# First keys and queries loaded in three pieces of heads, a planner with transfers at 270 GB/s, and inverse sums of two blocks also on ScalarE

## The chip, the cores and the metric

The program runs on one core of a Trainium2 chip. The metric is the time of one execution on the device in microseconds (us). The kernel before took 1215.35 us (median of three runs, 1214.6 to 1215.85). The execution that the profiler recorded took 1215.45 us; the trace of its instructions spans 1213.3 us of them, so 2.15 us lie outside the trace.

## What is computed

Three stages follow one another, each on the output of the stage before:

```python
# 1. attention in chunks: batch 4, heads 8, 768 tokens, head width 64, 8 memory tokens
for c in range(nc):                       # a chunk has 32 queries
    k_full = concat([mem_k, k[l_start:r_end]])      # 16 keys to the left, 8 to the right
    scores = scale * q_c @ k_full.T
    a = exp(scores - max(scores)); a = a / (sum(a) + 1e-9)
    out[c] = a @ v_full
x = out as (3072 tokens, 512)
# 2. first layer:  h = x @ w_in (512 x 2048); g = h * tanh(softplus(h)); x1 = g @ w_out
# 3. second layer: the same shapes, with g = h * sigmoid(1.702 h)
```

The weights come as 64-bit floats and are turned into 32-bit numbers on the chip.

## The kernel before

**Blocks.** Tokens are worked on in blocks of 384. Block `j` has 8 *quads* of attention: a quad is two heads by two groups of 96 queries. For blocks 0 and 1 (`EARLY = 2`) keys and queries are loaded with the tokens in the partitions (`rows_of_heads`, one call for four quads: all 8 heads of two groups of 96 queries) and turned on TensorE (`turned`, L665). Of each quad, in this order: TensorE turns queries and keys (L673) into a bank `h`; ScalarE or VectorE copies the bank to `qT` or `kT` (L680, L681); TensorE forms the scores (L708); VectorE adds the mask and finds the extreme (L721); ScalarE takes the exponential and the sums (L736); VectorE inverts the sums (L754, L758) and multiplies by them (`norm`, L761); TensorE turns the result (L782); it is copied to `aT` (L788, L789); TensorE multiplies by the values `vt` (L799 in block 0, L808 in later blocks); the output is split into a high and a low part, `xh` and `xl` (L834 to L840), the input of the first layer.

**First layer.** `step(j, f)` does one of 16 slices of the inner width: 12 matmuls into a bank `h` (L895, called the *first product* of slice `f` below), the activation on ScalarE (L907), and the products with `w_out` into four banks `o` (L924). Within block 0 the weights are still being converted: of each half of a slice ScalarE or VectorE takes the high word (L343, L346), and VectorE does three more steps (L352, L356, L360) and for `w_in` the split (L379, L384). The turned keys and the first products share two banks `h`. A weight load waits until the conversion six halves earlier has begun (`AHEAD`).

**Second layer.** `step2` does 7 products of 6 matmuls per pair of slices (L1057), with tanh on ScalarE (L1107), one step on VectorE (L1109) and the products of L1084.

**What sets the order.** Nothing is written in the order in which it runs. Every operation is added to a `Plan` with a rank, its reads and writes, and one or more *ways* (an engine, a duration, the function). `Plan.issue` (L139) then plays the program through with these durations: at each moment each free engine takes, of the operations whose inputs are there, the one of lowest rank. ScalarE takes first what needs no other activation table, and an operation that does (`other`) only when nothing else is ready. A transfer ends at `max(bus, end + 0.65) + size`, and its readers may start 0.9 later; `size` comes from `bus()`, 360 GB/s for runs of 512 bytes or more and half of it for shorter ones. The operations are then written out in the order of these planned starts, and on the chip each engine works through its own list strictly in that order, waiting where an input is not there yet. Transfers are issued by SyncE (SP); those of block 0's keys, queries and values may also be issued by GpSimd (POOL). SP's list is worked off in order as well, and a transfer that finds the queue full waits at its head.

Of the kernel before, what the change touches and what calls it, by code (L numbers as in the profile page):

```python
# [12 lines left out]
AF = mybir.ActivationFunctionType  # L13
# [5 lines left out]
EARLY = 2  # L19
# [62 lines left out]
class Plan:  # L82
# [2 lines left out]

    LAG = {"pe": 0.2, "act": 0.16, "dve": 0.13, "pool": 0.2}
    RELOAD = 1.4

    def __init__(self):
        self.ops = []  # L90
# [48 lines left out]
    def issue(self):  # L139
        engines = ("pe", "act", "dve", "pool", "sp")  # L140
        free = dict.fromkeys(engines, 0.0)
        ready = {e: [] for e in engines}
        load = dict.fromkeys(engines, 0.0)
        coming = []
        bus = 0.0
        for op in self.ops:
            if op.need == 0:
                heapq.heappush(coming, (0.0, op.seq, op))
            op.start = None
        left = len(self.ops)  # L150
        now = 0.0
        table = None
        order = []
        while left:
            while coming and coming[0][0] <= now + 1e-9:
                op = heapq.heappop(coming)[2]
                for w, (e, dur, *_) in enumerate(op.ways):
                    heapq.heappush(ready[e], (op.rank, op.seq, w, op))
                load[op.ways[0][0]] += op.ways[0][1]
            for e in engines:  # L160
                if free[e] > now + 1e-9:
                    continue
                kept = []
                pick = other = None
                while ready[e]:
                    item = heapq.heappop(ready[e])
                    op, w = item[3], item[2]
                    if op.start is not None:
                        continue
                    if w:  # L170

                        e0, d0 = op.ways[0][:2]
                        if max(free[e0] - now, 0.0) + load[e0] - d0 < op.ways[w][1] - d0 + 0.3:
                            kept.append(item)
                            continue
                    if e == "act" and op.table not in (None, table):

                        if other is None:
                            other = item
                        else:  # L180
                            kept.append(item)
                        continue
                    pick = item
                    break
                if pick is None:
                    pick = other
                elif other is not None:
                    kept.append(other)
                for item in kept:
                    heapq.heappush(ready[e], item)  # L190
                if pick is None:
                    continue
                op, w = pick[3], pick[2]
                e_, dur, fn, *size = op.ways[w]
                op.start, op.way = now, w
                load[op.ways[0][0]] -= op.ways[0][1]
                order.append(op)
                left -= 1
                end = now + dur
                if e == "act" and op.table not in (None, table):  # L200
                    if table is not None:
                        end += self.RELOAD
                    table = op.table
                free[e] = end
                lag = self.LAG.get(e, 0.0)
                if size:
                    bus = max(bus, end + 0.65) + size[0]
                    end, lag = bus, 0.9
                for o, far in op.after:
                    t = end + lag if far else (now + 0.01 if not size else now + 0.01)  # L210
                    o.at = max(o.at, t)
                    o.need -= 1
                    if o.need == 0:
                        heapq.heappush(coming, (o.at, o.seq, o))
            times = [coming[0][0]] if coming else []
            times += [free[e] for e in engines if free[e] > now + 1e-9]
            if not times:
                assert not left, "operations wait for one another"
                break
            now = min(t for t in times if t > now) if any(t > now for t in times) else now  # L220
        order.sort(key=lambda o: (o.start, o.seq))
        for op in order:
            op.ways[op.way][2]()


def dve(n, fast=False):
    return (170 + (0.53 if fast else 1.04) * n) / 1000


def act(n, psum=False):  # L230
    return ((180 if psum else 220) + 0.86 * n) / 1000


def bus(nbytes, run):
    return nbytes / 360e3 * (1 if run >= 512 else 2)


@with_exitstack
def kernel(
# [13 lines left out]
    nc = tc.nc  # L253
    B, H, S, D = q.shape
    NT, DM = out.shape
    DFF = w1_in.shape[1]
    NM = mem_k.shape[2]
    CHUNK, LEFT, RIGHT = 32, 16, 8
    P = 128
    KD = DM // P  # L260
    NF = DFF // P
    TB = 384
    NB = NT // TB
    GQ = 96
    NG = S // GQ
    GB = TB // GQ
    WIN = P - NM
# [6 lines left out]
    scale = 1.0 / float(D) ** 0.5  # L274
# [6 lines left out]
    add = plan.add  # L281
# [227 lines left out]
    ident = fixed(sb.tile([P, P], F32, name="ident"))  # L509
# [16 lines left out]
    def rows(src, r0, dims, col, width):  # L526

        return bass.AP(
            tensor=src.tensor, offset=src.offset + r0 * D + col, ap=[[st * D, n] for st, n in dims] + [[1, width]]
        )  # L530
# [91 lines left out]
        load(rank, vt, parts, P * GB * HV * D * 4, 256)  # L622
        return vt

    def windows(src, mem, b, t0, h0, nh, tile, i):


        runs = [(0, WIN, t0, 0, nh)]
        if b == 0 and h0 == 0 and t0 < 0:
            runs = [(0, WIN, t0, 1, nh - 1), (-t0, WIN + t0, 0, 0, 1), (0, -t0, 0, 0, 1)]  # L630
        elif b == B - 1 and h0 + nh == H and t0 + WIN > S:
            runs = [
                (0, WIN, t0, 0, nh - 1), (0, S - t0, t0, nh - 1, 1), (S - t0, t0 + WIN - S, t0, nh - 1, 1)
            ]
        parts = [
            lambda row=row, n=n, t=t, h=h, c=c: (
                tile[row:row + n, i, h:h + c],
                rows(src, (b * H + h0 + h) * S + t, [(1, n), (S, c)], 0, D),
            ) for row, n, t, h, c in runs
        ]  # L640
        parts.append(lambda: (tile[WIN:P, i], rows(mem, (b * H + h0) * NM, [(1, NM), (NM, nh)], 0, D)))
        return parts

    def rows_of_heads(j, gp, rank):

        b, s0 = divmod(j * TB, S)
        n = NF - 4 + 2 * j + gp
        qs, ks, vt = (T[nm].new([P, 2, H, D], F32) for nm in (f"wi{n}", f"wo{n}", "vt"))
        kp, vp = [], []
        for i in range(2):  # L650
            t0 = s0 + (2 * gp + i) * GQ - LEFT
            kp += windows(k, mem_k, b, t0, 0, H, ks, i)
            vp += windows(v, mem_v, b, t0, 0, H, vt, i)
        qp = [
            lambda i=i: (
                qs[:GQ, i], rows(q, b * H * S + s0 + (2 * gp + i) * GQ, [(1, GQ), (S, H)], 0, D)
            ) for i in range(2)
        ]
        size = P * 2 * H * D * 4
        load(rank - 4, ks, kp, size, 256, early=j == 0)  # L660
        load(rank - 4, qs, qp, size * GQ // P, 256, early=j == 0)
        load(rank - 2, vt, vp, size, 256, early=j == 0)
        return qs, ks, vt

    def turned(j, hp, st, rank):  # L665
        qs, ks, _ = st
        t = T["h"].new([P, 2 * (GQ + P)], F32)
        qk = T["qT" if hp % 2 else "kT"].new([P, 2 * (GQ + P)], F32)

        def turn():  # L670
            for i in range(2):
                for src, n, c in ((qs, GQ, i * GQ), (ks, P, 2 * GQ + i * P)):
                    nc.tensor.transpose(  # L673
                        t[:, c:c + n], src[:n, i, 2 * hp:2 * hp + 2].rearrange("p h d -> p (h d)"), ident[:n, :n]
                    )

        n = 2 * (GQ + P)
        add(rank, [("pe", 0.4, turn)], reads=[qs, ks, ident], writes=[t])
        add(rank, [
            ("act", act(n, True), lambda: nc.scalar.activation(out=qk[:, :n], in_=t.get(), func=AF.Copy)),  # L680
            ("dve", dve(n), lambda: nc.vector.tensor_copy(out=qk[:, :n], in_=t.get())),  # L681
        ], reads=[t], writes=[qk])
        return (
            lambda d, i: qk[d, i * GQ:(i + 1) * GQ],
            lambda d, i: qk[d, 2 * GQ + i * P:2 * GQ + (i + 1) * P],
            [qk],
        )

    def quad(j, hp, gp, heads, rank):
# [74 lines left out]

        add(rank + 1.4, [("dve", 0.23, plus)], reads=[sm], writes=[r])
        add(rank + 1.4, [("dve", 0.16, inverse)], updates=[r])
        add(rank + 1.4, [("dve", dve(4 * P), norm)], reads=[r, done], updates=[e])

        return after, e

# [484 lines left out]
```

## Time and profile before

| What | Value |
|---|---|
| median of 3 runs | 1215.35 us (1214.6 to 1215.85) |
| profiled execution, its span | 1215.45 us, 1213.3 us |
| TensorE (PE) busy | 1183.9 us, 98%, 6656 matmuls |
| its weight loads (PEld) | 1082.8 us, 89% |
| VectorE (DVE) busy | 822.5 us, 68% |
| ScalarE (ACT) busy | 564.9 us, 47% |
| GpSimd (POOL) busy | 10.1 us, 1% |
| mean granted clock of TensorE | 0.989 of 2.4 GHz |

How to read it: a busy share is an average over the whole span. A row of the windows gives, for a stretch, how long each engine was busy (and with how many instructions), the granted clock of TensorE (1.00 is 2.4 GHz, 0.50 is 1.2 GHz) and what the 16 DMA engines moved. A row of the waits says which engine stood still at which line, until which engine was done with what: total us, times, longest. A row of the timeline gives a start, a duration, and in brackets the idle time before it and what ended it. A bank or tile keeps its name without its number.

### The profile page before, as it was taken

To read this page: it belongs to the slowest core of one execution; us is meant where nothing else is said; L and a number is where in the kernel's file an instruction comes from. 1 tells how busy PE (TensorE), PEld (TensorE's weight loads), DVE (VectorE), ACT (ScalarE), POOL (GpSimd) and SP (SyncE) were. 2 spreads that over 40 slices of the span, in tenths; PEclk is the share of its full clock that TensorE was granted. 3 is DMA by queue.
4 is the path that set the end of the run, shared out by engine and by line. 5 is a ranking of instruction groups with operands and counts; after the bars stand their busy time and mean duration, and the time that the engine had idled before them with its cause. 6 is when DMAs were issued, how large, how long until landed. Compare 5 with 4: busy or idle time off the path is not lost.

```text
span 1213.3 us, 19142 instructions
## 1 busy us (share of the span) xinstructions
PE 1183.9 (98%) x6656; PEld 1082.8 (89%) x6656; DVE 822.5 (68%) x2379; ACT 564.9 (47%) x1303; POOL 10.1 (1%) x27
## 2 busy tenths in 40 slices
PE   7689999999999999999999999999999999999998
PEld 6567789999999999999999998998889888988897
DVE  5798878776866767667665668877655855555554
ACT  4677666655555555655533344445212521232112
POOL 1000000000000000000000000000000000000000
PEclk8799999999999999999999999999999999999999
DMA  9965545533433333334212676699656865566521
GB/s 204 262 216 168 147 124 139 147 94 80 114 88 92 98 91 93 103 81 116 60 49 74 229 257 209 231 356 335 214 186 194 296 226 189 179 224 214 181 106 53
DMA packets 214687, 197.80 MB, mean 163 GB/s; under 512 B 133496, under 2 KB 176519, under 8 KB 214591
## 3 DMA queue, kind: packets, MB, share of 16 engines
q1 hardware_dynamic: 214239, 195.82, 53.0%
q0 software_dynamic: 352, 0.75, 0.4%
q8 instruction: 53, 0.87, 0.3%
q14 instruction: 43, 0.35, 0.1%
HBM read 148.29 MB, written 48.23 MB: 162 GB/s over the span
## 4 chain that ended last, share of the span: by engine, by line
PE 93%; DMA 3%; SPq 2%; DVE 1%; ACT 1%; issue 0%; ACTq 0%
PE h L895 22%; PE o L924 22%; PE h L1057 19%; PE o L1084 15%; PE s L1084 7%; PE s L808 3%; PE s L708 3%; SPq L299 2%; PE s L782 2%; DMA vt<-in_v_dram 1%; DMA wo<-in_moe_w_out_dram 0%; DMA wi<-in_q_dram 0%; DMA x1d<-ev 0%; DMA st<-w1d 0%; DMA w1d<-u 0%
## 5 line engine op out<-in xcount | busy, mean ns | idle before, releaser
L895 PE MATMUL h<-xh,wi 128*128 128x384 f32 x1024 | 269.0, 344 | 5.9 <-ACT qT L680 4.4
L924 PE MATMUL o<-gh,wo 128*128 128x384 f32 x896 | 240.6, 349 | 0.0
L895 PEld LDWEIGHTS h<-xh,wi 128*128 128x128 f32 x1024 | 184.3, 189 | 13.2 <-ACT qT L680 5.2
L895 PE MATMUL h<-xl,wi 128*128 128x384 f32 x512 | 172.9, 338 | 0.0
L924 PEld LDWEIGHTS o<-gh,wo 128*128 128x128 f32 x896 | 158.0, 188 | 2.8
L924 PE MATMUL o<-gl,wo 128*128 128x384 f32 x448 | 150.8, 337 | 0.0
L907 ACT ACTIVATE u<-h 128x384 f32<-128x384 f32 x112 | 55.0, 491 | 132.0 <-PE h L895 125.5
L736 ACT ACTIVATE e<-e,mx 96x128 f32<-96x128 f32 x240 | 94.0, 393 | 23.5 <-DVE mx L721 22.9
L944 DVE TENSOR_TENSOR gl<-u,gh 128x384 fp32r<-128x384 f32 x177 | 96.9, 554 | 11.4 <-ACT gh L939 8.6
L895 PEld LDWEIGHTS h<-xl,wi 128*128 128x128 f32 x512 | 96.7, 189 | 0.0
L1057 PE MATMUL h<-wi,wi 128*128 128x384 f32 x480 | 94.4, 337 | 0.0
L1057 PEld LDWEIGHTS h<-wi,wi 128*128 128x128 f32 x480 | 85.5, 188 | 4.9 <-ACT v L1124 0.2
L924 PEld LDWEIGHTS o<-gl,wo 128*128 128x128 f32 x448 | 84.1, 188 | 0.0
L1124 ACT ACTIVATE v<-h 128x384 f32<-128x384 f32 x61 | 29.9, 490 | 113.2 <-PE h L1057 113.2
L1084 PE MATMUL o<-wo,gh 128*128 128x512 f32 x262 | 82.1, 394 | 0.2 <-ACT ev L951 0.2
L721 DVE CUSTOM_DVE_ANT_0 e<-s,mask 96x128 f32<-96x128 f32 x240 | 55.7, 283 | 37.5 <-PE s L708 36.4
L1057 PE MATMUL h<-wo,wi 128*128 128x384 f32 x384 | 77.2, 336 | 0.0
L907 ACT ACT_TABLE_LOAD x55 | 70.6, 1283 | 10.6 <-PE h L895 9.9
L1107 ACT ACTIVATE u<-e 128x384 f32<-128x384 f32 x64 | 33.5, 524 | 85.2 <-DVE e L1130 85.1
L736 ACT ACT_TABLE_LOAD x54 | 69.3, 1283 | 6.7 <-DVE mx L721 5.8
L1057 PEld LDWEIGHTS h<-wo,wi 128*128 128x128 f32 x384 | 68.2, 188 | 3.0 <-DVE u L1109 0.2
L836 DVE CAST xh<-s 64x192 fp32r<-64x192 f32 x84 | 29.8, 355 | 50.9 <-PE s L808 41.6
(195 smaller groups left out, 2057.8 us busy)
## 6 DMA issues: line engine op xcount, KB each, us to landing
wi<-w2c SPq DMA_DIRECT2D x72, 512.0 KB
wo<-w2o SPq DMA_DIRECT2D x48, 512.0 KB
w2c<-wi SPq DMA_DIRECT2D x24, 512.0 KB
st<-x1d SPq DMA_DIRECT2D x56, 192.0 KB
wi<-in_moe_w_in_dram SPq DMA_DIRECT2D x16, 512.0 KB
wo<-in_moe_w_out_dram SPq DMA_DIRECT2D x16, 512.0 KB
st<-in_moe_w_in_dram SPq DMA_DIRECT2D x16, 512.0 KB
w2d<-v SPq DMA_DIRECT2D x32, 256.0 KB
```

The lines of the kernel that those rows point to most:

```text
L708: nc.tensor.matmul(out=s[hh][:, i, :], lhsT=queries(d, i), rhs=keys(d, i), start=True, stop=True,)
L721: nc.vector.tensor_tensor_reduce(out=e[:, i, hh, :], in0=s[hh][:, i, :], in1=mask[:GQ, mask_of(g0 + i), :], scale=-scale, scalar=-NEG, op0 ...
L736: nc.scalar.activation(out=e[:, i, hh, :], in_=e[:, i, hh, :], func=AF.Exp, scale=-1.0, bias=mx[:, i, hh:hh + 1], accum_out=sm[:, i, hh:hh ...
L808: nc.tensor.matmul(out=o[:, i].rearrange("p h t -> p (h t)"), lhsT=vt[:, g + i, h:h + 2].rearrange("p h d -> p (h d)"), rhs=aT[:, i].rearr ...
L895: nc.tensor.matmul(out=h.get(), lhsT=a[:, c], rhs=b[:, kk, :], start=(n == 0), stop=(n == 3 * KD - 1))
L907: add(i + 0.3, [("act", act(TB, True), lambda: nc.scalar.activation(out=u.get(), in_=h.get(), func=AF.Mish))], reads=[h], writes=[u], tabl ...
L924: nc.tensor.matmul(out=o.get(), lhsT=a[:, c], rhs=b.get(), start=(first and n == 0), stop=(last and n == len(prods) - 1),)
L944: add(rank + 0.05, [("dve", dve(TB), lambda: nc.vector.tensor_tensor(out=gl.get(), in0=u.get(), in1=gh.get(), op=ALU.subtract))], reads=[u ...
L1057: nc.tensor.matmul(out=bank.get(), lhsT=a, rhs=b, start=(fresh and m == 0), stop=(m == 3 * K2 - 1), skip_group_check=not fresh,)
L1084: nc.tensor.matmul(out=o.get(), lhsT=a[:, c], rhs=w[:, b:b + DM], start=(first and k == 0), stop=(last and k == 2))
L1107: add(rank, [("act", act(TB, True), lambda: nc.scalar.activation(out=u.get(), in_=src(), func=AF.Tanh, scale=0.851))], reads=[src.buf], wr ...
L1124: ("act", act(TB, True), lambda: nc.scalar.activation(out=dst.get(), in_=bank.get(), func=AF.Copy)),
```

## The change

Four edits, in one program.

1. `rows_of_heads`: the first call (block 0, first two groups of queries) loads keys and queries in three pieces, heads 0 and 1, heads 2 and 3, heads 4 to 7; each piece is an object of its own, so a quad waits only for its own piece. The other calls keep one piece. The loads of the values are recorded behind the keys and queries of their call.
2. The planner's transfers: 270 GB/s for runs of 512 bytes or more (360 before), 180 for runs from 256 bytes (180 before), 108 below that (180 before); 0.9 and 1.1 us of fixed delay instead of 0.65 and 0.9.
3. The planner's choice on ScalarE: an operation that needs another table is taken at once when its rank is more than `PATIENCE = 1.0` below that of the operation that needs none.
4. `quad`: in blocks 0 and 1 the multiplication by the inverse sums may run on ScalarE, as four instructions (one for each head and group, scaled by a column), instead of the one on VectorE.

```diff
+    PATIENCE = 1.0
...
-                if pick is None:
-                    pick = other
-                elif other is not None:
+                if other is not None and (pick is None or other[0] + self.PATIENCE < pick[0]):
+                    pick, other = other, pick
+                if other is not None:
                     kept.append(other)
...
-                    bus = max(bus, end + 0.65) + size[0]
-                    end, lag = bus, 0.9
+                    bus = max(bus, end + 0.9) + size[0]
+                    end, lag = bus, 1.1
...
-    return nbytes / 360e3 * (1 if run >= 512 else 2)
+    return nbytes / 270e3 * (1 if run >= 512 else 1.5 if run >= 256 else 2.5)
...
+        cuts = (2, 4, H) if n == NF - 4 else (H,)
+        came, h0 = {}, 0
+        for h1 in cuts:
+            nh = h1 - h0
+            kp, qp = [], []
+            for i in range(2):
+                t0 = s0 + (2 * gp + i) * GQ
+                kp += windows(k, mem_k, b, t0 - LEFT, h0, nh, ks, i, h0)
+                qp.append(lambda i=i, t0=t0, h0=h0, nh=nh: (
+                    qs[:GQ, i, h0:h0 + nh], rows(q, (b * H + h0) * S + t0, [(1, GQ), (S, nh)], 0, D)
+                ))
+            some = Part(ks, 0, 0), Part(qs, 0, 0)
+            load(rank - 4, some[0], kp, size * nh // H, 256, early=j == 0)
+            load(rank - 4, some[1], qp, size * nh // H * GQ // P, 256, early=j == 0)
+            came.update({h: some for h in range(h0, h1)})
+            h0 = h1
...
-        add(rank, [("pe", 0.4, turn)], reads=[qs, ks, ident], writes=[t])
+        add(rank, [("pe", 0.4, turn)], reads=[*came[2 * hp], ident], writes=[t])
...
-        add(rank + 1.4, [("dve", dve(4 * P), norm)], reads=[r, done], updates=[e])
+        def norm_act():
+            for i in range(2):
+                for hh in range(2):
+                    nc.scalar.activation(
+                        out=e[:, i, hh, :], in_=e[:, i, hh, :], func=AF.Copy, scale=r[:, i, hh, :]
+                    )
+
+        ways = [("dve", dve(4 * P), norm), ("act", 4 * act(P), norm_act)]
+        add(rank + 1.4, ways if j < EARLY else ways[:1], reads=[r, done], updates=[e])
```

What this makes of the lists. TensorE has the same 6656 matmuls. In the whole program three of the sixteen multiplications by inverse sums of blocks 0 and 1 are put on ScalarE (the last quad of block 0 and the first two of block 1). Seventeen lines are added, so L895 becomes L912, L924 becomes L941, L808 becomes L825, L673 becomes L682. Three places matter.

The start of SP's list. `wo` here holds the first keys, `wi` the first queries, `vt` the values; a shape is partitions x heads x 64. Before:

```order
L299 DMA wo_87<-in_k_dram 120x7x64
L299 DMA wo_87<-in_k_dram 104x64
L299 DMA wo_87<-in_mem_k_dram 8x8x64
L299 DMA wo_87<-in_k_dram 120x8x64
L299 DMA wi_111<-in_q_dram 96x8x64 x2
L299 DMA vt<-in_v_dram 120x7x64
```

and now:

```order
L300 DMA wo_87<-in_k_dram 120x64
L300 DMA wo_87<-in_k_dram 104x64
L300 DMA wo_87<-in_mem_k_dram 8x2x64
L300 DMA wo_87<-in_k_dram 120x2x64
L300 DMA wi_111<-in_q_dram 96x2x64 x2
L300 DMA wo_87<-in_k_dram 120x2x64 x2
...
L300 DMA wo_87<-in_k_dram 120x4x64
L300 DMA wo_87<-in_mem_k_dram 8x4x64 x2
L300 DMA wi_111<-in_q_dram 96x4x64
L300 DMA vt<-in_v_dram 120x7x64
```

The eight transfers of the first keys and queries have become twenty (nine of the twelve more on SP, three on POOL), and all of them stand before the values.

TensorE's list where the second half of block 0's attention begins (`wi_126`, `wo_121` before and `wi_173`, `wo_159` now are its queries and keys). Before:

```order
L708 MATMUL o_217<-qT 96x128
...
L782 MATMUL o_249<-ident,e 128x96 x4
L673 MATMUL h<-ident,wi_126 128x96
L673 MATMUL h<-ident,wo_121 128x128
...
L799 MATMUL o_279<-aT,vt 64x96 x4
```

and now:

```order
L717 MATMUL o_221<-qT 96x128
...
L799 MATMUL o_235<-ident,e 128x96 x4
L816 MATMUL o_256<-aT,vt 64x96 x4
L799 MATMUL o_272<-ident,ev 128x96 x4
L816 MATMUL o_295<-aT,vt 64x96 x4
L682 MATMUL h<-ident,wi_173 128x96
L682 MATMUL h<-ident,wo_159 128x128
```

Two quads are now turned and multiplied by their values before the turning that waits for the second half's keys and queries.

TensorE's list around the first product of slice 0 (`wi_552` before, `wi_589` now). `s_618` and `s_682` are the first outputs of block 1's attention, which need the values `vt` of block 1; `wi_258` and `wi_334` are block 1's second queries. Before:

```order
L799 MATMUL o_578<-aT,vt 64x96 x4
L673 MATMUL h<-ident,wi_258 128x96
...
L782 MATMUL s_602<-ident,e 128x96 x4
L808 MATMUL s_618<-aT,vt 128x192 x2
L895 MATMUL h<-xh,wi_552 128x384 x2
...
L708 MATMUL s_676<-kT 96x128
...
L782 MATMUL s_692<-ident,e 128x96 x4
L924 MATMUL o_701<-gh,u 128x384
L924 MATMUL o_708<-gh,u 128x384
L808 MATMUL s_713<-aT,vt 128x192 x2
L895 MATMUL h<-xh,wi_628 128x384 x2
```

and now:

```order
L816 MATMUL o_593<-aT,vt 64x96 x4
L799 MATMUL s_602<-ident,e 128x96 x4
L682 MATMUL h<-ident,wi_334 128x96
...
L912 MATMUL h<-xh,wi_589 128x384 x2
...
L825 MATMUL s_682<-aT,vt 128x192 x2
L941 MATMUL o_688<-gh,u 128x384
...
L717 MATMUL s_706<-kT 96x128
...
L799 MATMUL s_729<-ident,e 128x96 x4
L912 MATMUL h<-xh,wi_650 128x384 x2
```

The first product of slice 0 now stands before the first multiplication by block 1's values, and all four products of L941 of slice 0 stand before the first product of slice 1, where two stood. On SP's list the values of block 1's first half have moved ahead of the fourth slice's `w_in`, behind which they stood.

## Rows read from the trace of the kernel before

**Rows 1.** Windows: stretch, length; busy PE, PEld, DVE, ACT, POOL; clock; DMA; GB/s.

```profile
40.00:50.00 10.00, 4.45 (x20) 2.95 (x20) 6.79 (x22) 5.02 (x16) 0.00 (x0) 0.50 1.02 235
50.00:60.00 10.00, 8.11 (x35) 6.83 (x36) 5.90 (x19) 6.85 (x12) 0.00 (x0) 0.68 1.10 341
60.00:80.00 20.00, 18.58 (x96) 13.72 (x95) 18.84 (x50) 14.55 (x33) 0.00 (x0) 1.00 0.67 228
80.00:100.00 20.00, 15.44 (x83) 12.18 (x83) 17.78 (x50) 14.66 (x35) 0.00 (x0) 1.00 0.72 220
```

**Rows 2.** Waits of PE from 105 us to the end: total us, times, longest.

```profile
PE s L782 <- DVE mx L721: 1.0, 1, 1.0
PE o L1084 <- ACT ev L951: 0.2, 1, 0.2
```

**Rows 3.** Waits of PE from 40 to 105 us.

```profile
PE h L895 <- ACT qT L680: 4.4, 2, 3.1
PE o L924 <- ACT gh L907: 3.2, 1, 3.2
PE s L808 <- DMA vt<-in_mem_v_dram: 3.1, 1, 3.1
PE h L895 <- ACT gl L907: 1.4, 1, 1.4
```

**Rows 4.** Timeline of PE, 45 to 60 us: start, duration, what, idle before.

```profile
45.55 0.98 PE L808 MATMUL s<-aT,vt 128*128 128x192 f32 x2 [3.08 <-DMA vt<-in_mem_v_dram]
47.16 1.01 PE L808 MATMUL s<-aT,vt 128*128 128x192 f32 x2 [0.64 <-DMA vt<-in_v_dram]
51.29 1.01 PE L895 MATMUL h<-xh,wi 128*128 128x384 f32 x2 [3.12 <-ACT qT L680]
...
55.43 1.15 PE L708 MATMUL s<-kT 64*96 64x128 f32 x8
57.17 0.55 PE L782 MATMUL s<-ident,e 96*128 96x96 f32 x4 [0.60 <-DVE mx L721]
57.56 1.48 PE L924 MATMUL o<-gh,u 128*128 128x384 f32 x4
...
59.40 0.65 PE L895 MATMUL h<-xh,wi 128*128 128x384 f32 x2
```

**Rows 5.** The chain that ended last, its two late landings.

```profile
34.55 4.90 DMA wi<-in_q_dram
41.26 5.86 DMA vt<-in_v_dram
```

**Rows 6.** Timeline of DVE, 36 to 70 us.

```profile
41.44 0.34 DVE L840 TENSOR_TENSOR xl<-o,xh 128x192 fp32r<-128x192 f32 x1
...
48.90 0.72 DVE L840 TENSOR_TENSOR xl<-s,xh 64x192 fp32r<-64x192 f32 x2 [2.85 <-ACT xh L834]
...
56.61 0.29 DVE L721 CUSTOM_DVE_ANT_0 e<-s,mask 96x128 f32<-96x128 f32 x1 [3.78 <-PE s L708]
...
69.66 0.68 DVE L384 TENSOR_TENSOR wi<-v,wi 128x512 fp32r<-128x512 f32 x1
```

**Rows 7.** Timeline of PE, the first scores.

```profile
10.65 0.68 PE L708 MATMUL s<-kT 64*96 64x128 f32 x8 [0.24 <-ACT kT L680]
```

**Rows 8.** Groups of 0 to 50 us: exponential on ACT, multiplication on DVE.

```profile
L736 ACT ACTIVATE e<-e,mx 96x128 f32<-96x128 f32 x24 | 9.3, 390 | 0.7 <-DVE mx L721 0.7
L761 DVE TENSOR_TENSOR e<-e,r 96x512 f32<-96x512 f32 x6 | 4.1, 682 | 0.0
```

**Rows 9.** DMA from 1.5 to 19.5 us: packets, and how many are short.

```profile
DMA packets 9754, 3.13 MB, mean 174 GB/s; under 512 B 9553, under 2 KB 9568, under 8 KB 9752
```

**Rows 10.** Issue of the 16 KB transfers, 0 to 40 us: ns, min/median/max.

```profile
L299 SPq DMA_DIRECT2D wo<-in_mem_k_dram x7: 298/1670/3548, 1.8 to 30.3; - x7
```

**Rows 11.** Timeline near the end: a gate of the second layer on ACT and DVE.

```profile
1190.39 0.49 ACT L1107 ACTIVATE u<-h 128x384 f32<-128x384 f32 x1 [3.65 <-PE h L1057]
1190.91 0.55 DVE L1109 SCALAR_TENSOR_TENSOR u<-u,h 128x384 f32<-128x384 f32 x1 [3.05 <-ACT u L1107]
```

More of the change, by code (lines that the diff above doesn't have):

```diff
@@ L623, in values_of, with windows @@
         return vt
-    def windows(src, mem, b, t0, h0, nh, tile, i):
+    def windows(src, mem, b, t0, h0, nh, tile, i, at=0):
         runs = [(0, WIN, t0, 0, nh)]
@@ L636, in windows @@
             lambda row=row, n=n, t=t, h=h, c=c: (
-                tile[row:row + n, i, h:h + c],
+                tile[row:row + n, i, at + h:at + h + c],
                 rows(src, (b * H + h0 + h) * S + t, [(1, n), (S, c)], 0, D),
@@ L640, in windows @@
         ]
-        parts.append(lambda: (tile[WIN:P, i], rows(mem, (b * H + h0) * NM, [(1, NM), (NM, nh)], 0, D)))
+        parts.append(lambda: (tile[WIN:P, i, at:at + nh], rows(mem, (b * H + h0) * NM, [(1, NM), (NM, nh)], 0, D)))
         return parts
@@ L648, in rows_of_heads @@
         qs, ks, vt = (T[nm].new([P, 2, H, D], F32) for nm in (f"wi{n}", f"wo{n}", "vt"))
-        kp, vp = [], []
-        for i in range(2):
[L651 to L661, printed above, removed]
+        size = P * 2 * H * D * 4
+        cuts = (2, 4, H) if n == NF - 4 else (H,)
[14 more added lines that the diff above has]
+            h0 = h1
+        vp = []
+        for i in range(2):
+            vp += windows(v, mem_v, b, s0 + (2 * gp + i) * GQ - LEFT, 0, H, vt, i)
         load(rank - 2, vt, vp, size, 256, early=j == 0)
-        return qs, ks, vt
+        return qs, ks, vt, came
     def turned(j, hp, st, rank):
-        qs, ks, _ = st
+        qs, ks, _, came = st
         t = T["h"].new([P, 2 * (GQ + P)], F32)
```

## The prediction

> **What bounds the kernel now.** I read the windows first, then the waits of TensorE, then its timeline where it waits, and last the chain and the other engines at that place. After 105 us TensorE waits twice in the whole rest of the span, 1.2 us together [rows 2]; it executes the same matmuls after the change, so this part can give nothing back and can only get worse. What can be won lies in the first 100 us. Between 40 and 60 us TensorE is busy 12.56 of 20 us, and the granted clock is 0.50 and 0.68; between 60 and 100 us it is busy 34.02 of 40 at clock 1.00, so 5.98 us are idle there [rows 1]. In those 40 us VectorE is busy 36.62, more than TensorE: it converts weights and is the other engine that sets the pace.
>
> The costliest place is 42 to 59 us. The input of the first layer for block 0 is complete at 41.44 + 0.34 = 41.8 us [rows 6], but the first product of slice 0 starts at 51.29 [rows 4]. In front of it on TensorE's list stands L808, block 1's first outputs, and that waits 3.08 us and again 0.64 for the values of block 1 [rows 4], whose last transfer is issued at 41.26 and lands at 47.12 [rows 5]. Behind it the first product waits 3.12 us more for a bank `h` that ScalarE copies out late [rows 3, 4]. VectorE stands behind the same instruction: 2.85 us until ScalarE has `xh`, then 3.78 us for scores that come after the first product [rows 6].
>
> **The change part by part.**
>
> *Pieces of the first keys.* The first scores start at 10.65 us [rows 7]. At the 174 GB/s of the first 18 us [rows 9], the 0.23 MB of a first piece take 1.3 us where the whole 0.92 MB take 5.3, so block 0 may begin up to 4.0 us earlier, and nothing earlier if the queue gives the pieces no lead. Is it on the path? The first product stands behind the turning of block 1's second queries, in both lists. These land at 34.55 + 4.90 = 39.45 us [rows 5] and have the same bytes ahead of them as before. With about 0.85 us for the turning, the first product starts at 40.3 at the earliest, and at 41.8 if block 0 is not a bit earlier. So the pieces alone are worth 0 to 1.5 us here, and what stands next decides whether even that counts: the values.
>
> *The list around the first product.* The first product now stands before the output that waits for the values. It takes 4.1 us at the low clock (51.29 to 55.43, [rows 4]) and ends at 44.4 to 45.9. The values of block 1 have lost one weight transfer of 512 KB from in front of them; at the 341 GB/s of 50 to 60 us [rows 1] that is 1.5 us, so they land at 45.6 instead of 47.1 (47.1 if transfers already in flight shared the engines anyway). The output then ends at 45.6 + 1.0 = 46.6, whether block 0 was early or not: the pieces are covered by the values. Then come four products of L924 (two take 1.48, so 3.0), scores (about 0.6 at the full clock, 1.15 at the low one) and a turning (0.55), and the first product of slice 1 [rows 4]. That makes 46.6 + 3.0 + 0.6 + 0.55 = 50.75 at the full clock, and 46.6 + 6.0 + 1.15 + 0.9 = 54.65 at the low one (the 0.9 for the turning is its 0.55 doubled, less overlap). The clock: the scores at 55.43 still take 1.15 us, the turning at 57.17 is at full speed again, so the engine came back from 0.50 once the first product's twelve matmuls and the scores had run nearly without a break [rows 4]. In the new list such work begins at 40.3, but a break of up to 2 us before the values follows it, so I take the middle, 52.5 us, against 59.40 before: 6.9 us earlier. At that point two products more are done (1.48) and one output less (0.65 at the full clock), which adds 0.8. Sum 7.7 us, with bounds of 9.5 (full clock) and 4.1 (low clock, values as late as before).
>
> *VectorE.* TensorE can't keep a lead that the conversions don't have. The split of slice 4 (L384) starts at 69.66 [rows 6]. Before, from 48.90 on, VectorE waits 3.78 us for scores; now these come right after three products of L924 and the wait is 1 us or so: 2.8 won. Its `xl` starts 1.3 us earlier, at about 47.6, since it hangs on the values. Five conversion steps that stood behind the `xl` of L840 now stand before it, where VectorE would wait for the values anyway; between five times 0.34 and five times 0.68 us (the shortest and the longest of such steps, [rows 6]), I take 2.5. That is 6.6 us. From 60 to 100 us VectorE idles only 3.4 of 40 us [rows 1], so it wins little more there. Between its 6.6 and TensorE's 7.7 I take **7.0 us** as what survives; the idle 5.98 us of TensorE from 60 to 100 I leave as it is (bounds: all of it gone, or 4 us more of it).
>
> *Multiplication on ScalarE.* Three times 0.68 us leave VectorE; ScalarE gets twelve instructions. No row shows one; the nearest is the exponential, 0.39 us each with a column operand [rows 8], so up to 4.7 us. ScalarE is busy 5.02 of 10 us from 40 to 50 [rows 1], and VectorE would spend what it gains waiting for the values. I take 0, with bounds of -2.0 and +1.5 (the activation of slice 0 late by what ScalarE can't place before it).
>
> *The later list.* The orders of TensorE agree in kind from 105 us to the end, with a few bunches in the second layer: up to 30 matmuls of L1057 in a row where 12 stood. There a bank must pass through a gate, 0.49 us on ScalarE and 0.55 on VectorE, 1.07 from start to end [rows 11], with one product instead of a block of L1084 in between to hide it. Two or three bunches, each between 0 and 1.07 us: I take +0.5 in all. A plan that holds transfers for slower than they are puts their readers later in the lists, so a wait for a load is less likely than before, not more.
>
> The sum, against the profiled execution (1213.3 of span and 2.15 around it, 1215.45; it lies 0.1 above the median of the runs): 1215.45 - 7.0 + 0.5 = **1208.9 us**. With the bounds above it runs from about 1205 to 1212.
>
> **The rivals.**
>
> *Bigger.* The 5.98 us between 60 and 100 us go too, because they come from TensorE and VectorE being out of step [rows 1, 3], and both now start this stretch less crowded: 1203. For it: 3.2 us of it is one wait for one activation on ScalarE [rows 3], behind a change of tables. Against: VectorE is nearly full there, and each of its steps is still needed.
>
> *Paid back.* TensorE gets the 7.7 us, but the conversions do not: the fourth slice's `w_in` is now behind the values on SP's list, and VectorE at 36.62 of 40 us has no room to catch up. Then only the earlier `xl` (1.3 us) or nothing is left when TensorE meets the conversions: 1212.5 to 1215.5. Also the case in which the change does not do what it says, since pieces and multiplications are covered.
>
> *Slower.* The loads are the bound up to 47 us, and there are more of them. SP issues nine transfers more before block 1's second queries. The 16 KB transfers of the same queue took 0.3 to 3.5 us each, 1.67 in the median [rows 10]. If each new piece costs as much, queries and values come 9 x 1.67 = 15.0 us later, the first product of slice 1 starts at 67.5 instead of 59.40, and the time is 1215.45 + 8.1 - 0.8 + 0.5 = 1223.2. It decides from 0.7 us for each transfer. Against it: 9553 of 9754 packets of the first 18 us are under 512 bytes [rows 9], heads are 256-byte rows in either form, so the number of packets stays; and the long issues come late, at a full queue, while the shortest, 0.3 us, is the first one at 1.8 us, where the new pieces stand. The Trainium skill speaks for this rival: "DMA: Bandwidth & Descriptors", section Rules for kernel authors, advises to put small transfers together, since below 64 KB they are mostly overhead, and the new pieces of two heads have 60 KB of keys and 48 KB of queries. Its fixed cost of about 2.0 us (section Anatomy of one DMA) would make, as an estimate, 12 x 2.0 = 24 us if no two pieces overlapped, a time near 1232; no run here shows it yet.
>
> **How the numbers follow.** Forecast 0.52, bigger 0.12, paid back 0.22, slower 0.14. A measurement of this kernel tells about 0.2% (2.4 us) from no change, so faster is below 1212.9 and slower above 1217.8. Of paid back I count 0.10 as just faster and 0.12 as the same. That gives faster 0.74, same 0.12, slower 0.14. The range reaches from the bigger rival, 1203, to 1215, which leaves out the slower one and a little more.
>
> **What would show it.** Right: the first product of slice 0 (L912) between 40 and 43 us; block 1's first output (L825) waits for the values until 45 to 47; the first product of slice 1 at 50 to 54; the split of slice 4 near 63; TensorE full from about 92 us; waits after that of 2 us at most. Wrong: block 1's second queries landing after 42 us (slower); the split of slice 4 still near 69 (paid back); new waits in the second layer above 3 us; a clock of 0.50 that lasts beyond 58.

## The result, and the profile after

The changed kernel takes 1204.59 us (median of 4 runs, 1203.5 to 1205.73); the kernel before took 1215.51 beside it. The ratio is 0.9911, 95% interval [0.9894, 0.9929]: 10.9 us less. The forecast was 1208.9, so direction and range hold, and the gain is 1.7 times the 6.5 us that were forecast. The profiled execution took 1205.73 us, its span is 1204.0, 9.3 us less than before.

Windows of the kernel after (stretch, length; busy PE, PEld, DVE, ACT, POOL; clock; DMA; GB/s), to be read against [rows 1]:

```profile
0.00:100.00 100.00, 86.60 (x542) 68.23 (x543) 82.44 (x294) 68.90 (x194) 7.67 (x17) 0.91 0.89 240
100.00:200.00 100.00, 98.19 (x556) 84.86 (x554) 85.35 (x256) 67.97 (x151) 1.14 (x4) 1.00 0.52 138
...
40.00:50.00 10.00, 9.56 (x34) 7.34 (x34) 8.90 (x24) 6.61 (x14) 0.00 (x0) 0.69 0.92 205
50.00:60.00 10.00, 8.03 (x44) 7.36 (x44) 9.39 (x24) 6.62 (x15) 0.00 (x0) 0.83 1.06 350
60.00:80.00 20.00, 20.00 (x100) 15.17 (x99) 16.62 (x49) 16.22 (x35) 0.00 (x0) 1.00 0.78 256
80.00:100.00 20.00, 20.00 (x107) 15.68 (x106) 18.31 (x52) 13.62 (x28) 0.00 (x0) 1.00 0.83 261
```

The same view of the kernel before, the first two hundred us:

```profile
0.00:100.00 100.00, 75.92 (x478) 59.34 (x479) 75.63 (x273) 63.17 (x180) 5.99 (x14) 0.86 0.88 229
100.00:200.00 100.00, 98.95 (x550) 84.08 (x549) 82.89 (x250) 65.78 (x145) 0.92 (x3) 1.00 0.51 140
```

TensorE's idle time in the first 100 us falls from 24.08 to 13.40, by 10.7. From 100 to 200 us it is 0.8 longer, and its busy time over the span grows by 0.8 (1183.9 to 1184.7). That makes 9.1 of the span's 9.3. The 5.98 idle us between 60 and 100 are all gone.

TensorE's waits after, 40 to 105 us and then from 105 to the end, against [rows 3] and [rows 2]:

```profile
PE h L912 <- ACT gl L924: 1.9, 1, 1.9
PE h L682 <- DMA wi<-in_q_dram: 0.6, 1, 0.6
...
PE o L941 <- DVE u L361: 1.3, 1, 1.3
PE h L912 <- DVE wi L385: 0.6, 1, 0.6
```

No wait for values is left, and none for the bank copied to `qT`; what remains is mainly one wait for `gl`, the activation of slice 1. The later list costs 1.9 us of waits where 1.2 stood.

TensorE's timeline after, against [rows 7] and [rows 4]:

```profile
8.11 0.68 PE L717 MATMUL s<-kT 64*96 64x128 f32 x8 [0.63 <-ACT kT L689]
...
40.06 0.42 PE L682 MATMUL h<-ident,wi 96*128 96x96 f32 x1 [0.59 <-DMA wi<-in_q_dram]
...
40.84 1.01 PE L912 MATMUL h<-xh,wi 128*128 128x384 f32 x2
...
44.85 1.48 PE L825 MATMUL s<-aT,vt 128*128 128x192 f32 x4
46.12 2.19 PE L941 MATMUL o<-gh,u 128*128 128x384 f32 x6
48.24 0.68 PE L717 MATMUL s<-kT 64*96 64x128 f32 x8
...
50.38 0.60 PE L912 MATMUL h<-xh,wi 128*128 128x384 f32 x2
...
55.71 0.62 PE L912 MATMUL h<-xh,wi 128*128 128x384 f32 x2 [1.93 <-ACT gl L924]
```

The first scores start at 8.11 (10.65 before), the first product of slice 0 at 40.84 (51.29), the scores behind it at 48.24 (55.43), slice 1 at 50.38 (59.40), slice 2 at 55.71 (65.65).

VectorE's and ScalarE's timelines after, against [rows 6] and [rows 8]:

```profile
38.67 0.35 DVE L857 TENSOR_TENSOR xl<-o,xh 128x192 fp32r<-128x192 f32 x1
...
62.02 0.69 DVE L385 TENSOR_TENSOR wi<-v,wi 128x512 fp32r<-128x512 f32 x1
```

```profile
41.48 1.28 ACT L779 ACTIVATE e<-e,r 96x128 f32<-96x128 f32 x4 [0.69 <-DVE r L767]
```

Block 0's input is complete at 39.0 (41.8), the split of slice 4 starts at 62.02 (69.66). The four multiplications on ScalarE take 1.28 us together, for the 0.68 of VectorE's one [rows 8].

The chain that ended last, after (start, duration, what), then before at the same place of the program:

```profile
42.67 6.96 DMA wi<-in_moe_w_in_dram
...
49.65 0.67 ACT v L344
...
50.35 0.54 ACT kT L689
...
50.91 1.28 ACT L745
...
52.20 1.65 ACT e L745 x8
...
53.87 1.28 ACT L924
...
55.16 0.50 ACT gl L924
...
55.71 3.56 PE h L912 x12
```

```profile
55.50 1.13 PE s L708 x8
...
63.82 0.47 ACT L907
...
65.11 0.50 ACT gl L907
...
65.65 2.37 PE h L895 x12
```

From 49.65 to 55.66 the chain is ScalarE alone: a conversion that waited for a weight transfer, the turned keys, a table load of 1.28, four exponentials, a second load, `gl`. In both kernels the chain reaches slice 2 through `gl` of slice 1, ten us apart (55.16 and 65.11). This path has no term in the prediction's sum.

### The profile page after: what moved, and what is told of

It reads as the page before. It is cut to its first block, busy times and chain, and to the rows that moved or that the text cites. A ratio compares the mean times of both kernels' runs of the same rounds, so it can differ in the third digit from the quotient of the medians.

```text
span 1204.0 us, 19160 instructions
## 1 busy us (share of the span) xinstructions
PE 1184.7 (98%) x6656; PEld 1084.7 (90%) x6656; DVE 822.8 (68%) x2375; ACT 563.7 (47%) x1313; POOL 12.4 (1%) x33
## 4 chain that ended last, share of the span: by engine, by line
PE 94%; SPq 3%; DMA 1%; DVE 1%; ACT 1%; issue 0%; ACTq 0%
PE o L941 23%; PE h L912 22%; PE h L1074 20%; PE o L1101 15%; PE s L1101 7%; PE s L825 3%; PE s L717 3%; SPq L300 3%; PE s L799 1%; DMA wi<-in_moe_w_in_dram 1%; DMA kl<-in_k_dram 0%; DMA wo<-in_k_dram 0%; ACT e L745 0%; DVE u L361 0%; ACT L924 0%
## 5 line engine op out<-in xcount | busy, mean ns | idle before, releaser
L912 PE MATMUL h<-xh,wi 128*128 128x384 f32 x1024 | 273.2, 348 | 2.6 <-ACT gl L924 1.9
L941 PE MATMUL o<-gh,wo 128*128 128x384 f32 x896 | 239.7, 348 | 0.0
L912 PEld LDWEIGHTS h<-xh,wi 128*128 128x128 f32 x1024 | 184.5, 189 | 11.7 <-ACT gl L924 2.1
L912 PE MATMUL h<-xl,wi 128*128 128x384 f32 x512 | 173.7, 339 | 0.0
L941 PEld LDWEIGHTS o<-gh,wo 128*128 128x128 f32 x896 | 158.8, 188 | 1.4
L941 PE MATMUL o<-gl,wo 128*128 128x384 f32 x448 | 150.8, 337 | 0.0
L924 ACT ACTIVATE u<-h 128x384 f32<-128x384 f32 x112 | 54.9, 490 | 131.1 <-PE h L912 124.5
L912 PEld LDWEIGHTS h<-xl,wi 128*128 128x128 f32 x512 | 97.1, 190 | 0.0
L941 PEld LDWEIGHTS o<-gl,wo 128*128 128x128 f32 x448 | 84.1, 188 | 0.0
L1126 DVE SCALAR_TENSOR_TENSOR u<-u,h 128x384 f32<-128x384 f32 x32 | 17.7, 554 | 63.1 <-ACT u L1124 63.1
```

What stands on the lines that cost most here:

```text
L912: nc.tensor.matmul(out=h.get(), lhsT=a[:, c], rhs=b[:, kk, :], start=(n == 0), stop=(n == 3 * KD - 1))
L924: add(i + 0.3, [("act", act(TB, True), lambda: nc.scalar.activation(out=u.get(), in_=h.get(), func=AF.Mish))], reads=[h], writes=[u], tabl ...
L941: nc.tensor.matmul(out=o.get(), lhsT=a[:, c], rhs=b.get(), start=(first and n == 0), stop=(last and n == len(prods) - 1),)
```

## The experiments

Each kernel was timed beside the kernel before, on one of three chips; the kernel before had medians of 1214.92, 1216.91 and 1215.64 us there. A ratio is always to the kernel before on the same chip. The edits are numbered as in the change: 1 pieces, 2 transfers, 3 patience, 4 multiplication. The planner's list follows from each edit, so none moves one instruction alone.

### The first product ahead of the values, and nothing else

The kernel before, with the planner alone told that block 1's first values take longer:

```diff
-        load(rank - 2, vt, vp, size, 256, early=j == 0)
+        load(rank - 2, vt, vp, size * (2.5 if (j, gp) == (1, 0) else 1), 256, early=j == 0)
```

> The kernel before, in which the planner alone is told that the values of block 1's first half take 2.5 times as long; the transfers themselves are as before. TensorE's list is that of before up to the first product of slice 0, which now stands ahead of the first output of block 1; there are no pieces, no ScalarE multiplication, no slower transfers otherwise. Theory 'place' (what was won is the first product no longer standing behind the wait for the values): first product near 42 us instead of 51.29, 1206 to 1209 us. Theory 'early start' (the pieces begin block 0 earlier, and that lead is carried through): no pieces, so 1214 to 1216. Theory 'transfers' (a plan with slower transfers as a whole makes better lists everywhere): 1213 to 1216.

Measured 1211.36 us, 0.9975 [0.9965, 0.9985]. TensorE's wait at the first product is another one:

```profile
PE h L895 <- ACT qT L680: 4.8, 1, 4.8
```

The product stands ahead of the values and starts at 44.91, slice 1 at 53.90; but slice 4 is only 3.1 us ahead of before. The place alone brings 0.25 of the 0.89%.

### Each edit alone

```diff
# pieces_only: the kernel before with
+        cuts = (2, 4, H) if n == NF - 4 else (H,)
# act_mult_only: the kernel before with
+        add(rank + 1.4, ways if j < EARLY else ways[:1], reads=[r, done], updates=[e])
# patience_only: the kernel before with
+                if other is not None and (pick is None or other[0] + self.PATIENCE < pick[0]):
```

> The kernel before with the three pieces of the first keys and queries alone. Its list has the first product ahead of the first output of block 1. 'Place': 1205 to 1208. 'Early start': 1205 to 1208 as well. 'Transfers': 1213 to 1216.

> The kernel before with the multiplications that ScalarE may take, alone (three are put there). The output of block 1 stands ahead of the first product. 'Place': 1212 to 1216. A theory by which relief of VectorE counts (3 x 0.68 us): 1212 to 1213.5. 'Early start' and 'transfers': 1214 to 1216.

> The kernel before with the new table rule alone. 'Patience': 1209 to 1212, with the waits of TensorE for activations from 40 to 105 us (4.6 us before) mostly gone. 'Relief': 1213 to 1216.

Measured 0.9974 [0.9964, 0.9985], 0.9976 [0.9964, 0.9988] and 0.9969 [0.9957, 0.9982]: about 3 us each. With the pieces alone the first product starts at 42.77, 8.5 us sooner than before, yet TensorE then waits, and reaches slice 4 only 4.4 sooner:

```profile
PE h L903 <- ACT gl L915: 3.3, 2, 2.9
PE o L932 <- ACT gh L915: 1.3, 1, 1.3
```

So most of the early product's lead is paid back in waits for ScalarE. The multiplication, which the prediction took as 0, and patience, which had no term, bring as much as the pieces.

### Each edit left out of the changed kernel

```diff
# no_act_mult
+        add(rank + 1.4, ways[:1], reads=[r, done], updates=[e])
# no_patience
-                if other is not None and (pick is None or other[0] + self.PATIENCE < pick[0]):
# old_transfers
+                    bus = max(bus, end + 0.65) + size[0]
+                    end, lag = bus, 0.9
+    return nbytes / 360e3 * (1 if run >= 512 else 2)
# no_pieces
+        cuts = (H,)
```

> The changed kernel without the multiplications on ScalarE: all sixteen stay on VectorE. The list of TensorE is as in the changed kernel up to the second slice. 'Place' fell short in the first four runs (1211.4 with the first product moved alone; 1207.4 with the values still in front), so I now ask what carries the lead past slice 3. Theory 'relief' (VectorE's and ScalarE's share of the quads is what lets the activation of slice 0 follow its product at once): 1208 to 1212, with the activation of slice 0 later than in the changed kernel (45.1 us). Theory 'patience' (the table rule does that): 1204 to 1206.

> The changed kernel with the old table rule of ScalarE. 'Relief': 1204 to 1207, since pieces, multiplications and place are all there. 'Patience': 1208 to 1212, with waits of TensorE for activations between 45 and 100 us as before (4.6 us).

> The changed kernel with the planner's old transfers (360 GB/s, delays 0.65 and 0.9): pieces, patience and ScalarE multiplications stay (eight of them instead of three), but the first output of block 1 stands ahead of the first product again. 'Place': 1211 to 1216, with a wait of TensorE for the values of about 3 us and the first product at 48 to 51. 'Early start': 1204 to 1207. 'Transfers': 1213 to 1216.

> The changed kernel with the first keys and queries in one piece. Its list has the values ahead of the first product. If edits add up (multiplication alone won 2.9 us in 1214.9, pieces alone 3.2): 1207 to 1209. If pieces are covered by the landing of values and queries, as I predicted: 1204 to 1206. If nothing works without them: 1212 to 1215.

Measured 0.9922 [0.9907, 0.9937], 0.9940 [0.9925, 0.9955], 0.9937 [0.9922, 0.9951], and without pieces 0.9874 [0.9859, 0.9888], 1201.51 us. Against 0.9911 for the whole, leaving out transfers or patience costs 0.26 or 0.29% (their intervals still overlap that of the whole by a little); the 0.11% of the multiplication is within the intervals; leaving out the pieces wins 0.37%. With the old transfers the values stand ahead of the first product again and TensorE waits 3.9 us for them, but 60 to 100 us is nearly full all the same:

```profile
60.00:80.00 20.00, 20.00 (x103) 15.34 (x104) 18.83 (x54) 16.69 (x39) 0.00 (x0) 1.00 0.85 294
80.00:100.00 20.00, 19.08 (x100) 14.93 (x99) 17.64 (x48) 14.26 (x30) 0.00 (x0) 1.00 0.68 214
```

Without pieces too the values stand in front. The two lists that keep the values where they were win 0.63 and 1.26%; late_values and pieces_only, whose lists move the product past them, 0.25 and 0.26%. These pairs differ in more than the place: act_mult_only and patience_only keep the values in front too and win 0.24 and 0.31%. So the place does not sort the kernels; np_late below moves it by itself, as far as the planner allows.

### The place put back into the best list, and the edits added up

```diff
# no_pieces_again: the changed kernel with
+        cuts = (H,)
# np_late: no_pieces_again with
+        load(rank - 2, vt, vp, size * (2.5 if (j, gp) == (1, 0) else 1), 256, early=j == 0)
# b_patnorm: the kernel before with edits 3 and 4
```

> The changed kernel once more, beside the three others of this call, so that its distance to the version without pieces is read on one chip. 'Pieces cost': 0.989 to 0.993 of the kernel before, and the version without pieces 2 to 5 us below it. 'Another chip's chance': the two within 1 us of each other.

> The changed kernel with the first keys and queries in one piece. 'Pieces cost': about 0.987 of the kernel before, 2 to 5 us below the changed kernel of this call, although its first first-layer product starts near 44.4 instead of 40.8. 'Place' (the term of the prediction: every us that this product starts sooner is a us won): it would have to be 3 us slower than the changed kernel, which the run before this one already spoke against.

> The version without pieces, and the planner alone is told that the values of block 1's first half take 2.5 times as long, so that the list puts the first product of slice 0 ahead of the output that needs them; the later list is the same. 'Place': the product starts near 42 instead of 44.4, and the run is 2 to 3 us faster than the version without pieces. 'Standing of the activation' (what decides is how soon the activation of each of the first slices comes behind its product, so that the next slices and the second output of slice 0 are not late): the lead is used up by slice 3, and the run is the same within 1 us, or slower by up to 3 where the output that is put behind the product then holds up the next slice.

> The kernel before with the planner's patience and the multiplication on ScalarE (four of the bunches there), transfers as before and keys and queries in one piece. 'Additive': the two alone gave 0.9969 and 0.9976, together 0.9945 (1208.5 against 1215.2). 'The list decides as a whole': between 0.993 and 0.998, and told by the first products of slices 0 to 5: where the lead at slice 4 is over 8 us (as in the versions that filled 60 to 100 us) it is near 0.993, where it is about 4 us near 0.997.

All four on one chip: changed 1205.3 us, 0.9919 [0.9902, 0.9935]; without pieces 1202.24, 0.9890 [0.9876, 0.9905]; without pieces and with the product ahead of the values 1208.79, 0.9946 [0.9932, 0.9959]; edits 3 and 4 on the kernel before 1209.3, 0.9944 [0.9928, 0.9959].

One number of the planner moves the first product 3.6 us forward (44.68 to 41.10) and makes the kernel 6.5 us slower. That refutes the place as what carries the gain: in the list that the planner makes of it, it costs. The chain of the slower one, then of the faster:

```profile
44.77 1.26 ACT e L779 x4
...
46.06 1.28 ACT L924
...
47.35 0.50 ACT gh L924
...
47.89 4.54 PE o L941 x8
52.44 0.66 PE s L717 x8
```

```profile
45.13 3.84 PE h L912 x12
48.97 0.66 PE s L717 x8
...
51.41 1.28 ACT L745
...
54.38 1.28 ACT L924
...
55.67 0.50 ACT gl L924
...
56.22 2.37 PE h L912 x12
```

In the slower list eight products of L941 stand between slice 0 and block 1's next scores. They wait for `gh`, which itself stands behind four multiplications and a table load, and then take 4.54 us, with a granted clock of 0.62 in that stretch (eight at full speed take 2.58, as at 66.13 in the changed kernel). The scores start at 52.4 instead of 48.9, and `gl`, which needs the exponentials of these scores out of ScalarE's way, at 57.94 instead of 55.67. In the faster list the scores follow the product at once. This accounts for 2.3 of the 6.5 us: slice 2 starts 3.9 us later than in the faster list and slice 4 6.5 later, and TensorE waits 4.5 us for `gh` in all, three times. What is lost behind slice 1 was not taken apart.

The sum of edits 3 and 4 is additive: 0.9969 x 0.9976 = 0.9945. The other theory there had tied 0.993 to a lead of over 8 us at slice 4; the lead was 9.4, but the profiled execution (1205.88) was the fastest of its six, so that test is weak. In steps on this chip: edits 3 and 4 take 6.3 us, edit 2 another 7.1 (1209.3 to 1202.24), and edit 1 gives 3.1 back. The pieces cost 3.1 us on this chip, where no run of the one kernel reaches those of the other (1204.28 at the least, 1203.72 at the most), though the two intervals overlap by a little; in the first pair the ratios are 0.37% apart and the intervals do not meet.

Most of this cost does not arise in the first 100 us. Counted in order of time through the blocks, slice 32 is the first of the third block and slice 127 the last of the first layer. Between their first products the kernel before and pieces_only have the same order of TensorE, and TensorE never waits. The windows of this stretch in the kernel before, from 230 us, and in pieces_only, from 225 us:

```profile
230.00:698.00 468.00, 468.00 (x2900) 451.70 (x2899) 318.71 (x1052) 251.69 (x571) 2.73 (x9) 1.00 0.36 98
```

```profile
225.00:695.00 470.00, 470.00 (x2901) 453.54 (x2900) 318.98 (x1053) 252.25 (x575) 2.74 (x9) 1.00 0.37 99
```

TensorE is busy all the time at a granted clock of 1.00. From the one first product to the other it takes 468.3 us (229.6 to 697.9) and 470.3 (224.7 to 695.0). The eight kernels without pieces take 468.2 to 468.3 us for this stretch, the six with pieces 469.6 to 470.3. The version with pieces, changed_again, is 0.3 us behind no_pieces_again at slice 32, 2.3 behind at slice 127, and 2.8 at the end. So the same matmuls run 0.4% slower in the kernels that load the first keys in pieces; no run here shows why.

All profiled executions together, in us from the span's start:

| kernel | ratio | first product, slice 0 | scores behind it | `gl` of slice 1 | first product, slice 4 |
|---|---|---|---|---|---|
| before | 1 | 51.3 | 55.4 | 65.1 | 79.8 |
| act_mult_only | 0.9976 | 46.0 | 50.2 | 60.5 | 74.7 |
| late_values | 0.9975 | 44.9 | 51.6 | 60.7 | 76.7 |
| pieces_only | 0.9974 | 42.8 | 54.5 | 61.7 | 75.4 |
| patience_only | 0.9969 | 49.6 | 53.5 | 64.7 | 79.4 |
| np_late | 0.9946 | 41.1 | 52.4 | 57.9 | 74.3 |
| b_patnorm | 0.9944 | 46.3 | 50.4 | 58.3 | 70.5 |
| no_patience | 0.9940 | 45.5 | 53.2 | 58.7 | 73.2 |
| old_transfers | 0.9937 | 45.5 | 49.7 | 57.0 | 69.2 |
| no_act_mult | 0.9922 | 42.4 | 49.3 | 57.7 | 75.0 |
| changed_again | 0.9919 | 43.4 | 50.1 | 55.7 | 68.7 |
| after | 0.9911 | 40.8 | 48.2 | 55.2 | 69.6 |
| no_pieces_again | 0.9890 | 44.7 | 48.9 | 55.7 | 67.8 |
| no_pieces | 0.9874 | 44.4 | 48.1 | 54.9 | 67.0 |

Against the time of the same execution the start of the first product has a correlation of 0.44 (0.16 without the row of before), the scores behind it 0.88 (0.83), `gl` of slice 1 0.87 (0.83), and a us of `gl` goes with 1.04 us of time. So the table sets the first product apart from the other two, but does not tell these two apart. The closest pair is act_mult_only and b_patnorm, which differ in patience: product and scores within 0.3 us of each other, `gl` 2.2 sooner, the ratio 0.32% lower. This is an ordering of whole lists, and no run moved `gl` by itself, so that it is the carrier stays a reading and is not shown. Changed_again and no_pieces_again have `gl` at 55.7 both and differ by 2.6 us; most of that is the slower pace behind slice 32. Patience_only does not fit either: `gl` and slice 4 are within 0.5 us of where they were, and its gain comes behind them (slice 9 starts 3.6 us sooner, slice 15 4.4).

## Why the prediction was right, and where it was not

**Where the time lies: right.** All of the gain arises in the first 100 us. The later list was put at +0.5 us for waits and shows 0.7 more waiting; that 1.9 us would be lost between slices 32 and 127 without any wait (11.1 us of lead at the one, 9.2 at the other) had no term.

**Pieces: right in the changed kernel's trace, wrong in worth.** Block 0 starts 2.5 us sooner and its input is complete 2.8 sooner, inside the bound of 4.0; the first product waits for block 1's queries, as forecast, at 40.06. Worth was put at 0 to 1.5 us. Alone they bring 3, and in the full list they cost 3: a cost that the bounds left out. Some 2 us of it are the slower pace from slice 32 to 127, whose reason stays open; pieces_only had won 4.9 us at slice 32 and keeps 2.9 at slice 127. The rest lies mainly in the early list: the two versions with pieces are 0.3 and 2.0 us behind those without at slice 32, and their second queries of block 1 are issued later (see the rival *slower*).

**Place: the step that failed.** "The first product now stands before the output that waits for the values" came about, and the times that followed from it came out: slice 1 at 50.38 and 52.07 in two executions (52.5, bounds 50.75 to 54.65), slice 4's split at 62.0 (63). But the 7.0 us were booked to that place. Moved alone it brings 3 us, put into the best list it costs 6.5. Agreement of the times had not shown the cause, and that the sum came out in its range is in part luck: this term stood in for gains of the other edits, which had none. The first product's start is not what the later slices hang on: the chain goes on through block 1's scores, the exponentials and two table loads to `gl`, and the working ended at slice 1 and handed over to VectorE. Two slips in the sum changed little: the middle of 50.75 and 54.65 is 52.7, and the bounds of all its terms reach further than "about 1205 to 1212" (those of TensorE's lead alone give 1206.5 to 1211.9, with the multiplication's and the later list's 1204 to 1216).

**VectorE: the carrier was named wrongly.** Its split of slice 4 came 7.6 us sooner (6.6 forecast), but as a follower: with a lead of about 10 us TensorE is full from 60 to 100 while VectorE is busy 34.93 of 40 us, less than before (36.62). So in this stretch it was not the limit of what survives.

**Multiplication and patience: mis-sized.** 0 was taken for the multiplication because VectorE would spend what it gains waiting for the values; it brings 2.9 us alone (0.24%, interval 0.12 to 0.36), at the middle past the bound of -2.0. Patience was not costed at all, and together they bring 6.3. The profile had shown the place: 3.2 us of wait for an activation behind a change of tables [rows 3], which I counted as an argument for a rival and not as a term.

**The rivals.** *Bigger* (1203) had its condition met: idle time from 60 to 100 us is 0.00. The result lies nearer to it than to the forecast. *Paid back* is refuted by the split at 62.02. *Slower* is refuted: block 1's second queries landed at 40.0, against 39.45 [rows 5], 0.6 us later and not the 6 us that 0.7 for each of nine would make. That is against another list, though. Against the same kernel without pieces the twelve transfers cost more: SP begins to issue these queries at 35.17 instead of 32.53 us, in the second pair at 34.49 instead of 32.90, so 2.6 and 1.6 us in all. The issues on SP, 0 to 20 us (ns, min/median/max), against [rows 10]:

```profile
L300 SPq DMA_DIRECT2D wo<-in_k_dram x9: 313/447/882, 0.7 to 19.8; - x9
...
L300 SPq DMA_DIRECT2D wi<-in_q_dram x5: 318/318/451, 2.4 to 13.5; - x5
```

That is 0.3 to 0.45 us each in the median, where 1.67 was taken from the 16 KB transfers up to 40 us. The Trainium skill's "DMA: Bandwidth & Descriptors", section Rules for kernel authors, counts transfers under 64 KB as mostly overhead; and the estimate of 24 us came from its fixed 2.0 us for each. The page gives that figure for transfers issued by GpSimd, while nine of the twelve more are on SP. The trace of after has this for a 48 KB piece on GpSimd (last: us from issue to landing):

```profile
wi<-in_q_dram POOLq DMA_DIRECT2D x1, 48.0 KB, 2.6
```

That agrees with a fixed time of such a size for one transfer; but twelve more transfers cost 1.6 to 2.6 us and not 24, so such times overlapped and did not add up.

## What to carry to other kernels

Where a planner writes the order, a predicted time that comes out does not show the predicted cause: change the one thing in the planner that makes that cause, and see whether the gain comes with it. Follow the chain past the instruction that moved, to the first engine that has to change what it does (here ScalarE between two activation tables); the lead is decided there. Compare also stretches far from the edit in which nothing waits: here 1.9 us are lost there, and no list of waits shows them. And leave each part out of a bundle once: one of the four edits cost 3 us, and the version without it, 1201.51 us, is the fastest of all.

## What the runs showed of the hardware

A table load took 1.28 us in the chains of the changed kernel, np_late and no_pieces_again, and in the changed kernel the next activation started right behind it (load at 53.87, `gl` at 55.16; the last exponential had ended at 53.85). The Trainium skill's "ScalarE: Activation LUTs", section What ACT_TABLE_LOAD costs, gives 1.28 for the load as well, and 2.66 with a drain; the chain has no such drain, and the trace decides: a switch costs 1.28 us here. The chain of the kernel before shows only 0.47 us of the load at 63.82, which lasts 1.28 in its timeline.

The granted clock differs between two executions of the same changed kernel. Window of the one, then of the other:

```profile
56.00:64.00 8.00, 8.00 (x41) 6.85 (x40) 6.19 (x19) 4.31 (x10) 0.00 (x0) 0.79 1.05 371
```

```profile
56.00:64.00 8.00, 7.79 (x44) 6.38 (x44) 7.89 (x24) 4.93 (x10) 0.00 (x0) 1.00 1.03 362
```

In the first TensorE had waited 1.93 us for `gl` before slice 2 and ran part of what followed at 1.2 GHz: that product took 3.56 us. In the second it had waited 0.74, stayed at 2.4 GHz and took 2.36. The length of the wait alone does not tell: the kernel before waited 1.42 us at this place and took 2.37 us, no_act_mult waited 1.01 and took 4.2, at a granted clock of 0.57 from 56 to 64 us. The first product of slice 0 also started 2.6 us later in the second (43.39), and its span is 1.0 us shorter: once more, the start of that product does not set the time. In no version shown did that product run at full speed: it took 4.21 us before, 3.84 without pieces, and 2.1 us is what a product at 2.4 GHz takes (slice 3, at 61.71). Whether these 2 us could be won, or would be taken back further on like the earlier start, no run shows.
